# Attention and Fourier mixing on one core: banks taken by their planned readers, left-over frequencies of two batches together, half of the k sums on GpSimd, block 1 loaded earlier

## The chip, the core and the metric

The kernel runs on one core of one Trainium2 chip. A core has TensorE (PE in the profile; its weight loads are shown as PEld), VectorE (DVE), ScalarE (ACT), GpSimd (POOL) and SyncE (SP), each with its own in-order queue of instructions. They share an on-chip memory of 128 partitions, the PSUM banks that matmuls write, and 16 DMA engines. The metric is the device time of one execution in microseconds, a median of several runs.

## The reference, cut to what matters

There are 8 batches of 576 positions, 8 heads of 64. Each batch has two attentions, one over groups of four positions (pooled) and one in a band of seven positions (local). Their sum x goes through a real part of a two-dimensional Fourier transform, a normalization and a two-layer network with residual.

```python
q_d = q.reshape(B, H, Sd, 4, D).mean(axis=3)        # k_d and v_d likewise; Sd = 144
out_up = np.repeat(sm_attn(q_d, k_d, v_d), 4, axis=2)
mask = np.abs(pos[:, None] - pos[None, :]) < 4      # local attention
x = out_up + softmax(where(mask, q k^T / 8, -1e9)) @ v
u = x + np.real(np.fft.fft(np.fft.fft(x, axis=1), axis=2))
un = (u - mean(u)) / sqrt(var(u) + 1e-6)            # over 512 channels
out = u + np.maximum(un @ w_ch1, 0) @ w_ch2         # 512 -> 2048 -> 512
```

The weights of the network come as 64-bit floats and are turned into pairs of 32-bit parts (a high one and the rest) on the chip; matmuls of the transform and of the network are done with such pairs, so each product takes three matmuls.

## The kernel before, in words

**Attention.** For each batch, five units of the local attention (class Unit) load a window of q and k (`qkT`), compute banded scores (`sc`), row maxima, exponentials (`sb`), transposes (`tpl`, `pT`), values (`av`) and write their result to one of two x tiles. Beside them four pairs of heads of the pooled attention (class Pooled) do the same on sums of four positions: `sums` (of q and k, L385, on VectorE, a reduction of each unit's `qkT`), scores `sp`, exponentials `sd`, transposes `tp`, values `avd`, output `odt`. The pooled v comes as four loads that add into `vsum`, three of them through GpSimd's queue, each waiting for the one before (L263).

**Mixing.** Class Mix turns a batch's x into the transform. GpSimd adds two halves of channels (`pq`, L514, in three buffers), VectorE folds them (`xeo`, L524 and L525), ScalarE and GpSimd split the result into a high and a low part (`fh`, `fl`, L539). TensorE applies the sequence transform (`y`, L559; `yz`, L575) to 290 frequencies, split again into `yh` and `yl`. Then `mix` (L597) applies the channel transform to the frequencies in slots of 128, 128 and 34 columns (`outs`); each slot is 13 matmuls, 6 of the odd and 7 of the even part. ScalarE copies the odd part (`copy_odd`), VectorE joins it with the even one (`join`, L609), and SyncE's queue stores the two results to `um` in DRAM (L615, L616).

**Network.** Class Block has 9 blocks of 512 tokens in four tiles `ut`. A block loads three parts: the local output `ul` (L700), two halves of the transform `um` (L688) and the pooled output `ud` (L685), the latter two added by the DMA. Statistics (L707 to L711), normalization `un` (L718), transposes `tpn` (L726) and a split into `unT` follow. `hps` (L755) is the first layer of one of 16 parts of the hidden size, `acc` (L773 to L775) the second. Weights are fetched in 64 quarters (`raw`, L157) and decoded by ScalarE (L167), GpSimd (L172), VectorE (L180 to L186), ScalarE (L197) and GpSimd (L201). The weights' places in memory become free as the attention ends, in steps (close_b, close_a, close_e, close_d). Blocks 0 and 1 first take five hidden parts each, while the rest of the weights is decoded.

**What sets the order.** Each step is put on a list with a due time, `at(t, fn)`, in planner's units: a batch every 20 units (`PACE`), and offsets from the table `AT`. The list is sorted by due time, and the instructions of all engines are issued in that order; each engine then works through its own in order and waits where data or a buffer is not there. PSUM banks (8 up to the crossing, 4 in the network, where `acc` has the others) are given out in rotation:

```python
def bank(name, rows=P):
    banks.append(banks.pop(0))
    return banks[-1].tile([P, DM], F32, name=name, tag="ps")[:rows]
```

The tiles of block 0 are in memory from the beginning, and its loads are due within batches 3 and 4. The tiles of block 1 take a place that the attention holds until its end (close_a), so its loads are due after it.

Of the kernel before, what the change touches and what calls it, by code (L numbers as in the profile page):

```python
# [20 lines left out]
PACE = 20  # L21
AT = {
    "pooled": (1.03, 0.13, -1.91, -2.96, -3.43),
    "mix": (18.91, 18.7, 18.08),
    "local_steps": (0, 1.57, 2.96, 4.76, 5.59, 7.95, 9.34),
    "pooled_steps": (0.2, 1.79, 3.0, 4.98, 5.63, 7.67, 9.22),
    "qk": (-12.1, 2.19),
    "sums": (-2.36, 0.34),
    "sum_v": (-12.66, -6.03, -4.76, 2.6),
    "load_v": (2.43,),  # L30
    "store_pooled": (0.1, 0.13),
    "crosses": ((1, 4.04), (2, 7.41), (0, 9.2)),
    "folds": ((3, 5.99), (1, 4.28), (2, 8.33), (0, 10.12)),
    "splits": (0.74, 0.9, 1.59),
    "z": (9.57, 11.56, 13.47, 16.06),
    "sequence": (12.92, 1.78, 0.82, 1.66),
    "mixed": (20.18, 2.55, 0.47, 0.7, 1.51, 2.55),
    "store_local": (9.66,),
    "ffn": (3.56, 1.64),
    "decode": (49.49, 9.91, 9.02, 1.2, 1.84),  # L40
    "decode_steps": (-1.47, -0.47, 0.83, 2.01, 2.96),
    "first_norms": (89.93, -0.58, 91.0, 4.0),
    "second_norms": (0.03, 1.47, 0.8, 1.93),
    "add": (0, 2.77, 2.2),
    "add0": (59.9, 3.96, 6.0),
    "early": (3.97, 1.76),
    "constants": (15.12, 26.0),
    "qk1": (-12.1, 2.19),
    "sum_v1": (-11.31, -6.45, -2.94, 2.35),
# [21 lines left out]
def kernel(  # L71
# [27 lines left out]
    NK1 = 290  # L99
    GX = G - W  # L100
# [17 lines left out]
    res.tile([P, 104], F32, name="gap")  # L118
# [17 lines left out]
    uts = {0: [res.tile([P, DM], F32, name=f"ut0{i}") for i in range(TILES)]}  # L136
    unTs = {0: res.tile([P, 2, NCC, TILES * P], F32R, name="unT0")}
    stat = ctx.enter_context(tc.tile_pool(name="stat", bufs=4))
    mhalf = res.tile([P, 25], F32, name="mhalf")[:, :1]
# [79 lines left out]
    pbank = ExitStack()  # L219
    banks = [ctx.enter_context(tc.tile_pool(name="banks", bufs=8 - TILES, space=PSUM))]  # L220
    banks.append(pbank.enter_context(tc.tile_pool(name="more_banks", bufs=TILES, space=PSUM)))
    first_bank = banks[:1]
    pools = {}

    def bank(name, rows=P):
        banks.append(banks.pop(0))
        return banks[-1].tile([P, DM], F32, name=name, tag="ps")[:rows]
# [823 lines left out]
```

## Time and profile before

| | |
|---|---|
| median of 3 runs (lowest, highest) | 1157.84 us (1153.98, 1159.70) |
| profiled execution, its own time | 1156.91 us |
| its span, first to last instruction | 1155.1 us |
| PE busy, share of the span | 1088.4 us, 94% |
| DVE, ACT, POOL busy | 529.5, 352.7, 323.2 us |
| mean granted clock of TensorE | 0.964 |

Matmuls are pipelined, so a busy TensorE is one that has matmuls under way. PEclk is the granted clock as a share of 2.4 GHz; it has two levels, 1.2 and 2.4 GHz, so a mean of 0.89 is a stretch with some time at the lower one. `a <- b` in a list of waits reads: the instruction a waited until b was done. The tiles' names in the rows are those of the code above.

### The profile page before, as it was taken

How to read it: one execution, taken by the hardware profiler on the slowest of the kernel's cores; microseconds unless marked ns; L12 is line 12 of the kernel's file. 1: busy time of each engine (PE TensorE's matmuls, PEld its weight loads, DVE VectorE, ACT ScalarE, POOL GpSimd, SP SyncE). 2: the span in 40 equal slices, each digit the busy share in tenths (PEclk: the TensorE clock that was granted, in tenths of full speed). 3: DMA queues.
4: the chain of work that ended last, by engine and by line, in shares of the span. 5: the costliest groups of instructions: out<-in, count | busy, mean ns of one | idle time of the engine just before them, and what ended most of it. 6: DMA issues, size and time to landing. Idle time of an engine off the chain costs nothing.

```text
span 1155.1 us, 20852 instructions
## 1 busy us (share of the span) xinstructions
PE 1088.4 (94%) x8304; PEld 917.1 (79%) x8304; DVE 529.5 (46%) x1218; ACT 352.7 (31%) x1046; POOL 323.2 (28%) x447
## 2 busy tenths in 40 slices
PE   4889898899986999999999999999999999999998
PEld 3778787788865888888888888888888888888887
DVE  3778879898658999232222232232222122132111
ACT  2657746766633444111111111111111111111110
POOL 2124654432285656403202102301300400400000
PEclk6789879999987999999999999999999999999999
DMA  9677798677385444604204303302401501500000
GB/s 272 192 233 240 205 233 246 192 187 212 107 216 116 137 126 119 129 17 104 43 1 98 49 1 89 58 1 72 75 0 58 90 1 44 102 1 21 16 1 36
DMA packets 64338, 119.45 MB, mean 103 GB/s; under 512 B 8845, under 2 KB 22813, under 8 KB 63986
## 3 DMA queue, kind: packets, MB, share of 16 engines
q1 hardware_dynamic: 44706, 87.50, 23.9%
q0 software_dynamic: 19536, 30.62, 15.9%
q8 instruction: 65, 1.06, 0.4%
q14 instruction: 31, 0.25, 0.1%
HBM read 89.92 MB, written 27.05 MB: 101 GB/s over the span
## 4 chain that ended last, share of the span: by engine, by line
PE 68%; DVE 2%; POOL 1%; DMA 1%; issue 1%; SPq 0%; ACT 0%; DVEq 0%; POOLq 0%; ACTq 0%
PE hps L755 33%; PE acc L775 11%; PE acc L773 11%; PE acc L774 11%; PE tpn L726 1%; DMA raw<-in_wq_dram 1%; POOL ut L688 1%; DVE wt L183 0%; DVE ut L779 0%; DVE st L707 0%; DVE wt L180 0%; DVE un L718 0%; DVE o L609 0%; DVE unT L735 0%; PE mix L597 0%
## 5 line engine op out<-in xcount | busy, mean ns | idle before, releaser
L763 DVE SCALAR_TENSOR_TENSOR hl<-hps,hh 128x512 fp32r<-128x512 f32 x144 | 99.4, 691 | 472.9 <-ACT hh L759 472.8
L755 PE MATMUL hps<-unT,w1h 128*128 128x512 f32 x1152 | 311.8, 393 | 0.0
L755 PEld LDWEIGHTS hps<-unT,w1h 128*128 128x128 f32 x1152 | 214.1, 188 | 43.9 <-ACT w1h L197 0.3
L759 ACT ACTIVATE hh<-hps 128x512 fp32r<-128x512 f32 x144 | 85.8, 596 | 522.1 <-PE hps L755 519.9
L773 PE MATMUL acc<-w2h,hh 128*128 128x512 f32 x576 | 224.7, 390 | 0.0
L775 PE MATMUL acc<-w2h,hl 128*128 128x512 f32 x576 | 224.3, 389 | 0.0
L774 PE MATMUL acc<-w2l,hh 128*128 128x512 f32 x576 | 224.2, 389 | 0.0
L755 PE MATMUL hps<-unT,w1l 128*128 128x512 f32 x576 | 154.5, 390 | 1.8 <-POOL w1l L201 1.8
L688 POOL DMA_DIRECT2D ut<-um x96 | 84.5, 1511 | 204.4 <-DMA ut<-ul 169.9
L755 PEld LDWEIGHTS hps<-unT,w1l 128*128 128x128 f32 x576 | 108.0, 188 | 25.1 <-POOL w1l L201 2.2
L775 PEld LDWEIGHTS acc<-w2h,hl 128*128 128x128 f32 x576 | 108.2, 188 | 22.7
L773 PEld LDWEIGHTS acc<-w2h,hh 128*128 128x128 f32 x576 | 108.2, 188 | 22.3
L774 PEld LDWEIGHTS acc<-w2l,hh 128*128 128x128 f32 x576 | 108.3, 188 | 22.3
L711 POOL TENSOR_TENSOR rstd<-rstd,mhalf 128x1 f32<-128x1 f32 x36 | 20.1, 559 | 272.5 <-DVE rstd L710 272.4
L419 ACT ACTIVATE sb<-sc,mx 128x64 f32<-128x64 f32 x320 | 69.8, 329 | 1.3
L319 PE MATMUL avd<-vsum,ptd 72*72 72x65 f32 x512 | 43.3, 243 | 8.6 <-DMA vsum<-in_vg_dram 6.8
L559 PE MATMUL y<-seqm,fh 128*128 128x290 f32 (+1 forms) x256 | 45.7, 323 | 5.4 <-ACT fh L532 3.5
L735 DVE TENSOR_TENSOR unT<-tpn,unT 128x512 fp32r<-128x512 f32 x36 | 24.8, 689 | 56.5 <-ACT unT L732 56.5
L319 PEld LDWEIGHTS avd<-vsum,ptd 72*72 72x72 f32 x512 | 41.7, 159 | 9.8 <-issue 9.0
L385 DVE TENSOR_REDUCE sums<-qkT 128x256 f32<-128x1024 f32 (+5 forms) x48 | 43.4, 946 | 11.1 <-DMA qkT<-in_qk_dram 10.4
L539 POOL TENSOR_TENSOR fl<-xeo,fh 128x512 fp32r<-128x512 f32 (+1 forms) x32 | 40.8, 1279 | 25.0 <-ACT fh L532 14.2
L685 POOL DMA_DIRECT2D ut<-ud x40 | 46.6, 1820 | 1.7 <-DMA ut<-um 1.3
(90 smaller groups left out, 1325.1 us busy)
## 6 DMA issues: line engine op xcount, KB each, us to landing
qkT<-in_qk_dram SPq DMA_DIRECT2D x40, 512.0 KB
raw<-in_wq_dram SPq DMA_DIRECT2D x64, 256.0 KB
vaug<-in_vw_dram SPq DMA_DIRECT2D x40, 260.0 KB
out_dram<-ut SPq DMA_DIRECT2D x36, 256.0 KB
ul<-x SPq DMA_DIRECT2D x8, 1024.0 KB
ut<-ud POOLq DMA_DIRECT2D x32, 256.0 KB, 6.6
vsum<-in_vg_dram POOLq DMA_DIRECT2D x24, 292.5 KB, 6.4
ut<-um POOLq DMA_DIRECT2D x48, 128.0 KB, 4.5
```

The costliest lines, as they stand in the source:

```text
L319: nc.tensor.matmul(av[:, t, hl, :], self.pts[h0][hl][:, kt, t * GH : (t + 1) * GH], self.vs[:, kt, h0 + hl, :], start=(kt == 0), stop=(kt ...
L385: nc.vector.tensor_reduce(out=to[:, :, g : g + n], in_=groups, axis=AX.X, op=ALU.add)
L419: nc.scalar.activation(out=self.sb[:, hp, h2], in_=sc[:, hp], func=AF.Exp, scale=0.125, bias=self.mx[:, h2, hp : hp + 1],)
L559: nc.tensor.matmul(y, l, r, start=(i == 0), stop=(i == len(mms) - 1))
L685: nc.gpsimd.dma_start(out=u[to : to + m], in_=groups, accum_op=ALU.add)
L688: nc.gpsimd.dma_start(out=u[to : to + m, h * HD : h * HD + HD], in_=um[b][i, k + j : k + j + m, z : z + HD], accum_op=ALU.add,)
L755: nc.tensor.matmul(hps, a[:, c, :], unT[:, x, c, :], start=(i == 0), stop=(i == len(mms) - 1))
L759: nc.scalar.activation(out=hh, in_=self.hps[f], func=AF.Relu)
L763: nc.vector.scalar_tensor_tensor(out=hl, in0=self.hps[f], scalar=0.0, in1=self.hh[f].bitcast(F32), op0=ALU.max, op1=ALU.subtract)
L773: nc.tensor.matmul(acc, hh, w2h, start=start, stop=False)
L774: nc.tensor.matmul(acc, hh, w2l, start=False, stop=False)
L775: nc.tensor.matmul(acc, hl, w2h, start=False, stop=stop)
```

## The change

1. **Banks.** Each of the eight banks is a pool of its own. `bank()` takes the one whose last planned reader is due first, which it looks up in the list of due times.
2. **Left-over frequencies.** An even batch mixes two slots of 128 and keeps its last 34 columns of `yh`, `yl` and `yz` at the front of the same tiles (`keep_rest`, three ScalarE copies). The odd batch behind it mixes two slots of 128 and one that holds both batches' rest. Its store writes the rest of both. `pq` has one buffer instead of three and `o` one instead of two.
3. **Sums of k.** From batch 2 on, the k half of `sums` is done by GpSimd in two additions for each group of columns, and the q half by VectorE in a reduction of half the size. In batches 0 and 1 VectorE does both, in two instructions.
4. **Block 1.** Its tiles `ut` are in memory from the beginning, as block 0's are; its loads and statistics are due within batches 4 to 6, its normalization after close_e as before.
5. **Start.** The mask and the identity in bf16 are ScalarE copies of a load in 32 bit by SyncE's queue; before, GpSimd's DMAs cast them.
6. **Table.** Nearly all offsets of `AT` are new, with own ones for batches 0 and 1; the constants' loads are split in two.

```diff
 PACE = 20
+POOL_SUMS = ((slice(0, 4), 0), (slice(4, 8), 1))
 AT = {
-    "mix": (18.91, 18.7, 18.08),
+    "mix": (19.06, 17.6, 18.13),
...
-    "mixed": (20.18, 2.55, 0.47, 0.7, 1.51, 2.55),
+    "mixed": (21.92, 2.32, 0.48, 0.57, 1.64, 2.55),
-    "add": (0, 2.77, 2.2),
-    "add0": (59.9, 3.96, 6.0),
+    "add0": (61.1, 1.15, 5.8),
+    "add1": (78.68, 3.12, 6.41),
+    "norms1": (127.29, 3.83, 1.92, 1.93),
...
-    uts = {0: [res.tile([P, DM], F32, name=f"ut0{i}") for i in range(TILES)]}
+    uts = {n: [res.tile([P, DM], F32, name=f"ut{n}{i}") for i in range(TILES)] for n in range(2)}
...
-    nc.gpsimd.dma_start(out=identb, in_=c_ident)
-    nc.gpsimd.dma_start(out=maskb, in_=c_mask)
+    mask = raws[0][:, P : 2 * P]
+    nc.sync.dma_start(out=mask, in_=c_mask.rearrange("p n w -> p (n w)"))
+    nc.scalar.copy(out=identb, in_=ident)
+    nc.scalar.copy(out=maskb.rearrange("p n w -> p (n w)"), in_=mask)
...
+    def read_until():
+        if now[0] is None:
+            return -1e8
+        owner, name, args = place(now[0])
+        if name == "mix":
+            return times[(owner, "copy_odd" if args[1] else "join", args[:1])]
+        return times[(owner, readers[name], args)]
+
     def bank(name, rows=P):
-        banks.append(banks.pop(0))
-        return banks[-1].tile([P, DM], F32, name=name, tag="ps")[:rows]
+        free = min(banks)
+        free[:2] = read_until(), len(events) + (bank_uses.append(name) or len(bank_uses))
+        return free[2].tile([P, DM], F32, name=name, tag="ps")[:rows]
...
-                nc.vector.tensor_reduce(out=to[:, :, g : g + n], in_=groups, axis=AX.X, op=ALU.add)
+                for h, pool in POOL_SUMS:
+                    if pool and self.b > 1:
+                        two = p2.tile([P, HP, 32, 2], F32, name="two", bufs=1)[:, :, :n]
+                        nc.gpsimd.tensor_tensor(out=two, in0=groups[:, h, :, 0:2], in1=groups[:, h, :, 2:4], op=ALU.add)
+                        nc.gpsimd.tensor_tensor(out=to[:, h, g : g + n], in0=two[:, :, :, 0], in1=two[:, :, :, 1], op=ALU.add)
+                    else:
+                        nc.vector.tensor_reduce(out=to[:, h, g : g + n], in_=groups[:, h], axis=AX.X, op=ALU.add)
...
+    places = [
+        [(REST, P), (REST + P, P)],
+        [(2 * REST - 1, P), (2 * REST - 1 + P, P), (0, 2 * REST - 1)],
+    ]
...
-            pq = self.pq[t] = psq.tile([P, 2, HD], F32, name="pq", bufs=3)
+            pq = self.pq[t] = psq.tile([P, 2, HD], F32, name="pq", bufs=1)
...
+        def keep_rest(self):
+            for y in (self.yh, self.yl):
+                nc.scalar.copy(out=y[:, :, :REST], in_=y[:, :, NK1:].bitcast(F32))
+            nc.scalar.copy(out=yz[:34, :REST], in_=yz[:34, NK1:].bitcast(F32))
...
-            n = outs[t]
-            cols = slice(P * t, P * t + n)
+            first, n = places[self.b % 2][t]
+            cols = slice(first, first + n)
...
-                STORE.dma_start(out=u[2 * P : HS + 1], in_=self.o[:n, i, NSL - 1])
+                if k:
+                    STORE.dma_start(out=um[self.b - 1][i, 2 * P : HS + 1], in_=self.o[:n, i, 2])
+                    STORE.dma_start(out=u[:n], in_=self.o[REST : REST + n, i, 2])
...
-            at(t_a + AT["add"][1] + 0.1 * i + AT["add"][2] * part, blocks[1].load, i, part)
+    for n, begin in enumerate((0.0, t_e)):
+        first, step, step_part = AT[f"add{n}"]
+        first_s, step_s, first_n, step_n = AT[f"norms{n}"]
+        for i in range(TILES):
+            for part in range(3):
+                at(first + step_part * part + step * i, blocks[n].load, i, part)
+            at(first_s + step_s * i, blocks[n].stats, i)
+            blocks[n].prepare_rest(i, begin + first_n + step_n * i)
```

Three places show how instructions move. The first is GpSimd's queue between batch 1's last low parts `fl` and batch 2's first cross sum `pq`. Before:

```order
L539 TENSOR_TENSOR fl<-xeo,fh 128x512
L172 TENSOR_SCALAR wt<-wt 128x256
L539 TENSOR_TENSOR fl<-xeo,fh 128x512
L263 DMA vsum<-in_vg_dram 72x1040 x2
L201 TENSOR_TENSOR w1l_86<-wt,w1h_85 128x256
L172 TENSOR_SCALAR wt<-wt 128x256
L263 DMA vsum<-in_vg_dram 72x1040
L700 DMA ut_95<-ul_65 61x512
L700 DMA ut_95<-ul_65 57x512
L700 DMA ut_95<-ul_65 10x512
L514 TENSOR_TENSOR pq<-x_134 128x256 x2
```

After (L433 and L434 are the new additions, `two` their intermediate):

```order
L213 TENSOR_TENSOR w1l_85<-wt,w1h_84 128x256
L308 DMA vsum<-in_vg_dram 72x1040
L433 TENSOR_TENSOR two<-qkT 128x256
L434 TENSOR_TENSOR sums<-two 128x4x32
L433 TENSOR_TENSOR two<-qkT 128x4x56
L434 TENSOR_TENSOR sums<-two 128x4x28
...
L433 TENSOR_TENSOR two<-qkT 128x4x54
L434 TENSOR_TENSOR sums<-two 128x4x27
L184 TENSOR_SCALAR wt<-wt 128x256
L308 DMA vsum<-in_vg_dram 72x1040
L771 DMA ut_94<-ul_65 61x512
```

Twelve additions now stand there, the k sums of batch 3, between two loads into `vsum`; block 0's first loads follow as before.

The second is TensorE's queue after the attention, from the first layer of hidden part 2 of block 0 to block 1's first transposes `tpn`. Before:

```order
L755 MATMUL hps<-unT_99,w1h_5921 128x512 x4
L755 MATMUL hps<-unT_99,w1l_5922 128x512 x4
L755 MATMUL hps<-unT_99,w1h_5921 128x512 x4
L726 MATMUL tpn<-ident,un 128x128 x4
L597 MATMUL mix<-chanm,yh 128x258 x2
L597 MATMUL mix<-chanm,yl 128x258
L597 MATMUL mix<-chanm,yh 128x258 x2
L597 MATMUL mix<-chanm,yl 128x258
```

After (`acc` at L847 to L849 is the second layer, `hps` at L829 the first, `mix` at L663):

```order
L829 MATMUL hps<-unT_102,w1h_6060 128x512 x4
L829 MATMUL hps<-unT_102,w1l_6061 128x512 x4
L829 MATMUL hps<-unT_102,w1h_6060 128x512 x4
L847 MATMUL acc<-w2h_90,hh 128x512
L848 MATMUL acc<-w2l_91,hh 128x512
L849 MATMUL acc<-w2h_90,hl 128x512
...
L848 MATMUL acc<-w2l_91,hh 128x512
L849 MATMUL acc<-w2h_90,hl 128x512
L797 MATMUL tpn<-ident,un 128x128 x4
L663 MATMUL mix<-chanm,yh 128x258 x2
```

The twelve second-layer matmuls of hidden part 1 now stand ahead of the transposes; before they stood behind them and a slot of the mixing.

The third is SyncE's queue at the same place. Before:

```order
L622 DMA ul_72<-x_135 128x4x512
L623 DMA ul_72<-x_135 64x2x512
L157 DMA raw<-in_wq_dram 128x512 x3
L700 DMA ut_5917<-ul_65 7x512
L700 DMA ut_5917<-ul_65 56x512
...
L700 DMA ut_5920<-ul_66 1x512
L157 DMA raw<-in_wq_dram 128x512 x12
L615 DMA um_80<-o 128x2x258
```

After (L682 to L685 store `um`, L169 fetches `raw` weights, L691 and L692 store the last batch's local output):

```order
L682 DMA um_79<-o 128x2x258 x2
L691 DMA ul_72<-x_157 128x4x512
L692 DMA ul_72<-x_157 64x2x512
L169 DMA raw<-in_wq_dram 128x512 x17
L682 DMA um_80<-o 128x2x258
L684 DMA um_79<-o 33x258
L685 DMA um_80<-o 33x258
```

The 21 loads of block 1's local part (the rows from L700 on, of which four stand here) are gone from between the weight fetches.

## Rows read from the trace of the kernel before

**Rows 1.** Busy time by stage: us, busy (instructions) of each engine, clock, DMA share, GB/s.

```profile
0.00:62.00 62.00, 40.15 (x732) 35.04 (x732) 35.72 (x94) 30.86 (x117) 17.22 (x32) 0.75 0.79 234
62.00:200.00 138.00, 122.40 (x1924) 108.35 (x1921) 110.36 (x303) 88.21 (x325) 65.67 (x89) 0.89 0.83 233
200.00:318.00 118.00, 107.59 (x1975) 96.70 (x1973) 98.51 (x286) 81.91 (x302) 39.08 (x51) 1.00 0.61 173
318.00:372.60 54.60, 39.79 (x205) 33.27 (x196) 35.36 (x79) 18.30 (x47) 39.30 (x56) 0.81 0.68 164
372.60:1149.00 776.40, 776.40 (x3479) 642.35 (x3478) 246.81 (x457) 133.39 (x256) 161.95 (x220) 1.00 0.24 55
```

**Rows 2.** The chain that ended last, in order of time: start, us, what.

```profile
372.86 2.77 PE hps L755 x12
378.35 2.72 PE hps L755 x12
...
1149.09 2.73 DVE ut L779 x4
```

**Rows 3.** TensorE's waits, 62 to 318 us: us in total, times, longest; first and last.

```profile
PE sp L274 <- DVE x L467: 2.8, 5, 0.7
...
PE y L559 <- ACT fh L532: 0.3, 1, 0.3
```

**Rows 4.** TensorE in order of time, start: start, us, what, [idle before <- releaser].

```profile
8.38 0.43 PE L394 MATMUL sc<-maskb,identb 64*64 64x256 bf16 x4 [3.61 <-DMA maskb<-in_c_mask_dram]
...
28.62 2.15 PE L319 MATMUL avd<-vsum,ptd 72*72 72x65 f32 x16 [6.75 <-DMA vsum<-in_vg_dram]
```

**Rows 5.** TensorE in order of time, batch 0's slot of 34.

```profile
93.81 0.42 PE L597 MATMUL mix<-chanm,yh 128*34 128x258 f32 x2
...
95.39 0.60 PE L431 MATMUL tpl<-ident,sb 128*128 128x128 f32 x4
```

**Rows 6.** Groups by line: busy, mean ns. VectorE's sums, all, largest and smallest form.

```profile
L385 DVE TENSOR_REDUCE sums<-qkT 128x256 f32<-128x1024 f32 (+5 forms) x48 | 43.4, 946 | 11.1 <-DMA qkT<-in_qk_dram 10.4 <-DMA vaug<-in_vw_dram 0.3 <-PE sp L274 0.2
L385 DVE TENSOR_REDUCE sums<-qkT 128x256 f32<-128x1024 f32 x8 | 9.8, 1220 | 6.0 <-DMA qkT<-in_qk_dram 5.4 <-DMA vaug<-in_vw_dram 0.3 <-PE sp L274 0.2
L385 DVE TENSOR_REDUCE sums<-qkT 128x96 f32<-128x384 f32 x8 | 4.4, 544 | 0.2 <-DMA qkT<-in_qk_dram 0.2
```

**Rows 7.** Groups by line and form: joins on 34 rows, statistics.

```profile
L609 DVE TENSOR_TENSOR o<-mix,o 34x258 f32<-34x258 f32 x16 | 6.7, 417 | 2.5 <-ACT o L603 2.1
L707 DVE BATCH_NORM_STATS2 st<-ut 128x6 f32<-128x512 f32 x36 | 24.6, 685 | 5.0 <-DMA raw<-in_wq_dram 5.0
```

**Rows 8.** GpSimd's additions by line: ns min/median/max, first and last start.

```profile
L514 POOL TENSOR_TENSOR pq<-x x48: 623/633/1382, 49.2 to 322.9; 128x256 f32<-128x256 f32 x48
L539 POOL TENSOR_TENSOR fl<-xeo,fh x32: 1253/1274/1410, 53.8 to 329.3; 128x512 fp32r<-128x512 f32 x24, 80x512 fp32r<-80x512 f32 x8
```

**Rows 9.** VectorE's folds by line: ns min/median/max.

```profile
L524 DVE TENSOR_TENSOR xeo<-pq x24: 406/418/1498, 50.4 to 325.3; 128x256 f32<-128x256 f32 x24
```

**Rows 10.** TensorE in order of time, crossing into the network.

```profile
344.84 1.59 PE L755 MATMUL hps<-unT,w1h 128*128 128x512 f32 x4
354.53 1.12 PE L726 MATMUL tpn<-ident,un 128*128 128x128 f32 x4 [8.10 <-DVE un L718]
```

**Rows 11.** GpSimd in order of time: first and last DMA issues of block 1.

```profile
331.34 5.21 POOL L688 DMA_DIRECT2D ut<-um  x6
...
344.11 4.82 POOL L685 DMA_DIRECT2D ut<-ud  x5
```

**Rows 12.** GpSimd in order of time: last decoding step, first and last of 45.

```profile
376.64 0.74 POOL L201 TENSOR_TENSOR w1l<-wt,w1h 128x256 fp32r<-128x256 f32 x1 [1.33 <-ACT w1h L197]
...
463.49 0.74 POOL L201 TENSOR_TENSOR w2l<-wt,w2h 128x256 fp32r<-128x256 f32 x1 [0.80 <-ACT w2h L197]
```

**Rows 13.** DMA issues: KB each, median us to landing.

```profile
ut<-um POOLq DMA_DIRECT2D x48, 128.0 KB, 4.5
```

**Rows 14.** TensorE in order of time: last scores of a batch, first of the next.

```profile
229.31 0.88 PE L274 MATMUL sp<-sums 64*72 64x144 f32 x8
...
242.40 0.71 PE L274 MATMUL sp<-sums 64*72 64x144 f32 x8 [0.70 <-DVE x L467]
```

More of the change, by code (lines that the diff above doesn't have):

```diff
@@ L99 @@
     NK1 = 290
+    REST = NK1 - 2 * P
     GX = G - W
@@ L219, with place @@
     pbank = ExitStack()
-    banks = [ctx.enter_context(tc.tile_pool(name="banks", bufs=8 - TILES, space=PSUM))]
-    banks.append(pbank.enter_context(tc.tile_pool(name="more_banks", bufs=TILES, space=PSUM)))
-    first_bank = banks[:1]
+    stacks = [ctx] * (8 - TILES) + [pbank] * TILES
+    banks = [[-1e9, i, x.enter_context(tc.tile_pool(name=f"bank{i}", bufs=1, space=PSUM))] for i, x in enumerate(stacks)]
+    first_banks = banks[: 8 - TILES]
     pools = {}
+    bank_uses, now = [], [None]
+    readers = {
+        "scores": "exps",
+        "transpose_p": "copy_p",
+        "values": "result",
+        "sequence": "sequence_low",
+        "sequence_z": "z_low",
+        "turn": "turn_low",
+        "first": "low",
+    }
+    times = {}
+    def place(fn):
+        return getattr(fn.func, "__self__", None), fn.func.__name__, fn.args
+    def read_until():
[5 more added lines that the diff above has]
+        return times[(owner, readers[name], args)]
     def bank(name, rows=P):
-        banks.append(banks.pop(0))
-        return banks[-1].tile([P, DM], F32, name=name, tag="ps")[:rows]
+        free = min(banks)
+        free[:2] = read_until(), len(events) + (bank_uses.append(name) or len(bank_uses))
+        return free[2].tile([P, DM], F32, name=name, tag="ps")[:rows]
     xab = [px.tile([P, NSL, 2, DM + 2], F32, name=f"x{i}") for i in range(2)]
@@ L636, in plan @@
-            at(t + AT["store_local"][0], self.store_local)
+                u = max(t + pace * u, moved if slot >= NSL - 1 else 0)
+                at(u + pace * fold, self.fold, slot)
+                at(u + pace * high, self.split_high, slot)
+                at(u + pace * low, self.split_low, slot)
+            at(t + pace * AT["store_local"][0], self.store_local)
             for d, fn in zip(AT["z"], (self.split_z, self.sequence_z, self.z_high, self.z_low)):
-                at(t + d, fn)
+                at(t + pace * d, fn)
@@ L639, in plan @@
             first, step, high, low = AT["sequence"]
             for T in range(4):
-                u = t + first + step * T
+                u = t + pace * (first + step * T)
                 at(u, self.sequence, T)
-                at(u + high, self.sequence_high, T)
-                at(u + low, self.sequence_low, T)
+                at(u + pace * high, self.sequence_high, T)
+                at(u + pace * low, self.sequence_low, T)
             first, step, even, copy, join, store = AT["mixed"]
-            for i in range(NSL):
-                u = t + first + step * i
+            if self.b % 2 == 0:
+                at(t + pace * AT["keep"][0], self.keep_rest)
@@ L648, in plan @@
+            for i in range(len(places[self.b % 2])):
+                u = t + pace * (first + step * i)
                 at(u, self.mix, i, 1)
-                at(u + even, self.mix, i, 0)
-                at(u + copy, self.copy_odd, i)
-                at(u + join, self.join, i)
-            at(u + store, self.store)
+                at(u + pace * even, self.mix, i, 0)
+                at(u + pace * copy, self.copy_odd, i)
+                at(u + pace * join, self.join, i)
+            at(u + pace * store, self.store)
@@ L834, in close_a @@
         pools["pt"] = pool("pt")
-        uts[1] = [pools["pt"].tile([P, DM], F32, name=f"ut1{i}") for i in range(TILES)]
         weight_tiles(pools["pt"], range(*CHUNKS[:2]))
         pbank.close()
-        banks[:] = first_bank
+        banks[:] = first_banks
         pacc[0] = pool("pacc", TILES, space=PSUM)
@@ L900 @@
     with tc.manual_schedule():
+        times.update((place(fn), t) for t, _n, fn in events)
         for _, _n, fn in sorted(events, key=lambda e: e[:2]):
+            now[0] = fn
             fn()
```

147 lines of the change are left out of this document (77 added, 70 removed).

## The prediction

> **What bounds the kernel now.** I read the busy times by stage first. They divide the run into a start (0 to 62 us), an attention part in two halves (62 to 200, 200 to 318), a crossing into the feed-forward network (318 to 372.6) and the network itself [rows 1]. The reader is to see that in the last stage TensorE is busy for all of its 776.4 us at clock 1.00. The chain of waits says the same: groups of 12 matmuls, 2.72 us each, one behind another up to the closing additions [rows 2]. 12 matmuls in 2.72 us are 0.227 us each, and the change takes none of them away. So whatever it brings must come out of the first 372.6 us.
>
> There TensorE stands still for 62 - 40.15 = 21.9 us in the start, (138 - 122.40) + (118 - 107.59) = 26.0 us in the attention, and 54.6 - 39.79 = 14.8 us in the crossing [rows 1]. It also runs slowly: the granted clock is 0.89 between 62 and 200 us. With its two levels, 1.2 and 2.4 GHz, that is 0.11 / 0.5 x 138 = 30 us at the lower one, against none between 200 and 318. VectorE is nearly as full as TensorE there (110.36 + 98.51 of 256 us, 82%). The list of TensorE's waits in the attention then tells who holds it up: 18 kinds of wait, the longest 2.8 us in total [rows 3]; 12 of the 18 name VectorE as the one that ended them, 17.0 us together. No single wait is worth much. The attention is four engines closely interleaved, and a gain must come from less work on the two full ones.
>
> **The change part by part.**
>
> *The left-over frequencies.* Before, each batch turns 290 frequencies in three slots of 128, 128 and 34 rows, and the slot of 34 costs 13 matmuls like a full one. At full clock it runs from 93.81 to 95.39, 1.58 us [rows 5]. Now an even batch has two slots and the odd one behind it three, so four of eight such slots go: 4 x 1.58 = **6.3 us** of TensorE, on the path. VectorE loses four pairs of joins on 34 rows, 8 x 0.417 = 3.3 us [rows 7]. ScalarE gains three small copies for each pair of batches and loses one; it is busy for (88.21 + 81.91) / 256 = 66% [rows 1], so I cost that at nothing, and at the 3 us it may take in all if ScalarE should be late.
>
> *The sums of k on GpSimd.* VectorE spends 43.4 us on 48 reductions, 5.43 us a batch [rows 6]. From the two ends, 1.220 us for 1024 elements and 0.544 for 384, an element costs 1.06 ns and an instruction 0.14. Half the elements of each then saves (5.43 - 6 x 0.14) / 2 = 2.3 us a batch, 13.8 us over six batches; batches 0 and 1 pay 6 x 0.14 each for the split, 1.7 us. Block 1's four statistics move into the attention, 4 x 0.685 = 2.7 us [rows 7]. VectorE's net relief is 13.8 + 3.3 - 1.7 - 2.7 = 12.7 us of the 209 that it is busy.
>
> How much of that reaches TensorE the trace doesn't show. Nothing is the lower bound, and the upper one is the 17.0 us of waits that VectorE ends. The new choice of PSUM banks (the bank whose planned last reader is earliest, in place of strict rotation) works on the same waits, since many of the 17 us are for a reader of an older tile. I take **8 us** for the two together, a little under half of the 17, since a wait that goes leaves the next one behind it.
>
> GpSimd takes on 12 additions a batch, 1152 + 576 = 1728 elements. Its addition of 256 elements takes 0.633 us and that of 512 takes 1.274 [rows 8], 2.5 ns an element, so 4.3 us a batch, or 6 us with some wait between dependent instructions. Is there room? The first scores of a batch follow the last ones of the batch before: 229.31 + 0.88 to 242.40 is 12.2 us [rows 14]. So in itself it is hidden. The cover goes where the instructions ahead of it in GpSimd's queue are late: the sums of batches 4 and 5 stand behind accumulating DMAs of blocks 0 and 1, of which six hold GpSimd for 5.21 us [rows 11] and each lands 4.5 us later [rows 13]. I charge **-6 us** for this, for the single buffer of pq (the next cross sum must wait for VectorE's fold), and for block 0's first read of the left-over rows, which the plan puts 0.4 of its units behind the store that writes them. Bounds: 0 and -40, the latter being a whole 6 to 7 us a batch on the path.
>
> One thing speaks against moving work to GpSimd: a fold on VectorE, 0.418 us as a rule, took 1.498 in one case [rows 9], with GpSimd's cross sums beside it. The Trainium skill states the reason on the page "SBUF — State Buffer", section "Who interferes with whom": a VectorE instruction with two SBUF inputs and a GpSimd one that reads SBUF exclude each other for the whole instruction. The trace agrees as far as that one row goes. By that rule the folds would pay wherever the sums stand beside them, and I make a rival of it below; the sum keeps the row's median, because in the new order the twelve additions stand between two batches' cross sums and folds, not among them.
>
> *The clock.* Between 200 and 318 us, with few idle gaps, it never fell; between 62 and 200 it was low for 30 us, in which TensorE could have done its work in half the time. The upper bound is 15 us, the lower 0. Fewer waits should take some of that; I take **5 us**.
>
> *The start.* The mask comes by SyncE's queue and a ScalarE copy instead of a casting DMA of GpSimd. TensorE's first wait for it was 3.61 us, and the longest of the start, 6.75 us, is for the accumulated v sums [rows 4]. In the new order more local work stands ahead of that wait: four units' scores, three transposes and two value products instead of three, one and one. But the DMA engines are busy for 0.79 of this stage [rows 1], and the loads are as many as before. I take **4 us**, bounds -3 and 12.
>
> *The crossing.* Before, the loads of block 1 wait for the end of the attention: GpSimd issues its DMAs from 331.34 until 344.11 + 4.82 = 348.9 [rows 11], its weight decoding waits between them, and TensorE, done at 344.84 + 1.59 = 346.4, starts block 1's first transposes at 354.53 after 8.10 us [rows 10]. From 346.4 to the next block's first group at 378.35 [rows 2] are 31.9 us. The work in it is 60 matmuls of the network (5 x 2.72 = 13.6), 39 of the mixing (39 x 1.58 / 13 = 4.7) and 16 short transposes (about 0.9): 19.2. So 12.7 us are idle or slow. With block 1 loaded long before, its statistics are there, and a group of 12 second-layer matmuls stands ahead of the transposes. What is late next is the decoding of weights: 45 quarters take from 376.64 to 463.49 when nothing is in their way, 1.97 us each [rows 12]. From 329 on, the 12 quarters of this round would be done by about 353, and TensorE needs the last of them some ten us after 346. So decoding should hold little. I take **10 us**, bounds 4 and 12.7.
>
> *The sum.* 6.3 + 8 - 6 + 5 + 4 + 10 = 27.3 us. The profiled execution took 1156.9 us (span 1155.1 and 1.8 around it; the median of the three runs, 1157.8, is 0.1% from it), so 1156.9 - 27.3 = **1130 us**. With the bounds of the parts near their better ends together it would be 1107, and with most near their worse ends 1145.
>
> **The rivals.**
>
> *A: the attention keeps its pace.* The in-order queues hand each freed wait to the next engine, so only the removed matmuls and the crossing count: 1156.9 - 6.3 - 10 + 3 = 1144. For it: the 18 small waits. Against it: VectorE is the releaser in most.
>
> *B: the clock stays up.* With most of VectorE's waits gone, TensorE never falls to 1.2 GHz in the attention: 13 of the 17 us, 12 of the 15, and the start's 8 instead of 4: 27.3 + 5 + 7 + 4 = 43 less, 1114. For it: the stretch from 200 to 318. Against it: twice the loads into the network's blocks in this part.
>
> *C: the shared port.* If GpSimd's additions do fall beside VectorE's eight folds a batch, and each waits as in the longest row, 8 x 1.08 x 6 = 52 us come onto VectorE in place of 12.7 off it. Half of the net 39 us on the path and the 8 us lost: 1130 + 8 + 19 = 1157.
>
> *D: slower.* GpSimd's sums come late at the first scores of every batch, since they stand behind DMAs that wait for landings. The price is the wait there, six times; from 27 / 6 = 4.5 us a batch on, all else is eaten up. At 7 us beyond my charge: 1130 + 42 = 1172. For it: the landings of 4.5 us that stand in the same queue [rows 13]. Against it: the 12.2 us of room [rows 14].
>
> *E: the change doesn't do what it says at the crossing*: decoding, not block 1, holds it. Then it returns 3 instead of 10: 1137, inside the forecast's own range.
>
> **How the numbers follow.** The forecast with E has 0.52 (its own range 1119 to 1140), A 0.18, B 0.13, C 0.07, D 0.10. For 8 in 10 I take 1108 to 1152: it leaves out D, most of C and the tail of B. About 0.5% is what a measurement of this kernel can tell from no change, here 5.8 us, so faster means under 1152. The forecast, A and B lie there but for a tail: 0.82. Between 1152 and 1163.6 lie most of C and the tails of A and D: 0.09. Slower: 0.09.
>
> **What would show it.** The network's part must again be about 776 us. The end of the attention (the last value products, at 318 before) should come near 301 us, and the dense part begin near 346 instead of 373. In the list of waits, TensorE's wait for VectorE's un of 8.10 us must be gone. VectorE's reductions must shrink to about 31 us, GpSimd's new additions sum to 26 to 40 us. The mixing must have 260 matmuls instead of 312. A wait of the first scores (sp) for GpSimd's sums of over 4 us in most batches would show D; folds with a median over 0.8 us would show C; an attention that still ends beyond 312 us would show A.

## The result and the profile after

The changed kernel takes 1142.3 us (median of 4 runs, 1139.9 to 1145.5) against 1157.6: a ratio of 0.987, 95% interval 0.983 to 0.991. That is faster by 15.3 us where 27.3 were forecast: inside the range, but nearer to rival A (1144) than to 1130. The profiled execution took 1144.4 us, with a span of 1142.3. One execution further below, of e11, took 3695 us where the others took 1140 to 1143, and its ratio leaves it out.

Busy time by stage, after, in the columns of [rows 1]:

```profile
0.00:62.00 62.00, 48.47 (x809) 40.17 (x810) 39.47 (x115) 35.40 (x133) 17.67 (x32) 0.83 0.89 273
62.00:200.00 138.00, 117.68 (x1895) 103.36 (x1895) 95.71 (x288) 85.36 (x317) 95.49 (x148) 0.90 0.86 230
200.00:318.00 118.00, 111.24 (x1878) 99.15 (x1879) 96.56 (x301) 83.61 (x309) 56.85 (x87) 0.94 0.68 185
318.00:360.00 42.00, 39.66 (x215) 34.19 (x214) 32.98 (x69) 19.34 (x50) 23.47 (x38) 0.96 0.50 150
360.00:1136.00 776.00, 773.12 (x3449) 637.39 (x3448) 238.93 (x447) 128.42 (x250) 159.74 (x216) 1.00 0.24 54
```

The reader is to see three things. In the crossing TensorE is now nearly always busy (39.66 of 42 us; before 39.79 of 54.6). In the attention VectorE is busy for 16.6 us less (192.27 against 208.87) and GpSimd for 47.6 more (152.34 against 104.75), yet TensorE idles as much as before: (138 - 117.68) + (118 - 111.24) = 27.1 us against 26.0. And its clock there is no better: 0.90 and 0.94 against 0.89 and 1.00.

TensorE in order of time, after, where [rows 10] stood: the first network matmuls behind the attention, the first transposes of block 1, and the group that stood at 378.35 [rows 2]:

```profile
316.08 1.20 PE L829 MATMUL hps<-unT,w1h 128*128 128x512 f32 x4
...
341.99 0.60 PE L797 MATMUL tpn<-ident,un 128*128 128x128 f32 x4
...
364.87 1.07 PE L829 MATMUL hps<-unT,w1h 128*128 128x512 f32 x4
```

The same two groups of network matmuls before, by the same view:

```profile
318.06 1.20 PE L755 MATMUL hps<-unT,w1h 128*128 128x512 f32 x4
...
378.19 1.07 PE L755 MATMUL hps<-unT,w1h 128*128 128x512 f32 x4
```

So the attention ends 2.0 us earlier and the crossing is 60.1 - 48.8 = 11.3 us shorter. The wait of 8.10 for `un` is gone; TensorE's waits from 312 to 380 us, after, are these two:

```profile
PE y L617 <- ACT fh L590: 1.5, 1, 1.5
PE yz L641 <- POOL z L606: 0.8, 1, 0.8
```

The rest of the span is the same to half a microsecond (777.4 against 776.9). The question is why the start and the attention, where 17 us were forecast together, gave 2.

TensorE's waits in the attention, 62 to 318 us, after (us in total, times, longest), to be held against [rows 3]:

```profile
PE y L617 <- POOL fl L597: 4.3, 2, 3.8
PE yz L641 <- POOL z L606: 3.8, 1, 3.8
PE tpn L797 <- DVE un L789: 3.0, 1, 3.0
PE sc L445 <- ACT sb L470: 3.0, 5, 1.1
...
PE sp L319 <- POOL sums L434: 0.6, 1, 0.6
```

GpSimd, which ended none of the 18 kinds of wait before, now ends 8.7 us of them. The sums that it took over are hardly among these (0.6 us); `fl` and `z` are, which were its work before too.

### The profile page after: what moved, and what is told of

The parts are those of the page before. It is cut to its first block, busy times and chain, and to the rows that moved or that the text cites. A ratio compares the mean times of both kernels' runs of the same rounds, so it can differ in the third digit from the quotient of the medians.

```text
span 1142.3 us, 20905 instructions
## 1 busy us (share of the span) xinstructions
PE 1092.7 (96%) x8252; PEld 916.1 (80%) x8252; DVE 506.4 (44%) x1222; ACT 352.1 (31%) x1057; POOL 353.2 (31%) x517
## 4 chain that ended last, share of the span: by engine, by line
PE 72%; DMA 12%; DVE 7%; POOL 4%; ACT 3%; issue 2%; SPq 1%; POOLq 0%; ACTq 0%; DVEq 0%
PE hps L829 30%; PE acc L849 10%; PE acc L847 10%; PE acc L848 10%; DMA raw<-in_wq_dram 4%; DMA vsum<-in_vg_dram 4%; DMA qkT<-in_qk_dram 2%; PE y L617 2%; PE mix L663 2%; PE tpn L797 1%; PE avd L364 1%; DMA ut<-um 1%; PE av L499 1%; DVE sums L436 1%; DVE x L518 1%
## 5 line engine op out<-in xcount | busy, mean ns | idle before, releaser
L829 PE MATMUL hps<-unT,w1h 128*128 128x512 f32 x1152 | 310.9, 392 | 0.0
L829 PEld LDWEIGHTS hps<-unT,w1h 128*128 128x128 f32 x1152 | 213.9, 188 | 43.1
L847 PE MATMUL acc<-w2h,hh 128*128 128x512 f32 x576 | 225.7, 392 | 2.9 <-DVE ut L853 2.8
L849 PE MATMUL acc<-w2h,hl 128*128 128x512 f32 x576 | 225.1, 391 | 0.0
L829 PE MATMUL hps<-unT,w1l 128*128 128x512 f32 x576 | 154.3, 390 | 0.0
L847 PEld LDWEIGHTS acc<-w2h,hh 128*128 128x128 f32 x576 | 108.5, 188 | 27.1 <-ACT w1h L209 2.0
L849 PEld LDWEIGHTS acc<-w2h,hl 128*128 128x128 f32 x576 | 108.5, 188 | 23.9 <-DVE hl L837 1.3
L829 PEld LDWEIGHTS hps<-unT,w1l 128*128 128x128 f32 x576 | 108.1, 188 | 23.1
L782 POOL TENSOR_TENSOR rstd<-rstd,mhalf 128x1 f32<-128x1 f32 x36 | 21.0, 643 | 265.6 <-DVE rstd L781 261.7
L597 POOL TENSOR_TENSOR fl<-xeo,fh 128x512 fp32r<-128x512 f32 (+1 forms) x32 | 44.9, 1411 | 23.6 <-ACT fh L590 21.6
L179 ACT ACTIVATE wt<-raw 128x256 f32<-128x256 f32 x64 | 28.1, 439 | 62.1 <-DMA raw<-in_wq_dram 44.9
L803 ACT CAST unT<-tpn 128x512 fp32r<-128x512 f32 x36 | 21.1, 587 | 82.0 <-PE tpn L797 82.0
```

Source lines behind the costliest of these rows:

```text
L597: nc.gpsimd.tensor_sub(out=l, in0=self.x[t], in1=h.bitcast(F32))
L829: nc.tensor.matmul(hps, a[:, c, :], unT[:, x, c, :], start=(i == 0), stop=(i == len(mms) - 1))
L847: nc.tensor.matmul(acc, hh, w2h, start=start, stop=False)
L849: nc.tensor.matmul(acc, hl, w2h, start=False, stop=stop)
```

## The experiments

In this table "end" is the start of the first network matmuls behind the attention and "crossing" the time from there to the group named above, by TensorE in order of time. Both are of one profiled execution each; the median and the ratio are of all. Ratios are to the kernel before, run on the same chip. e4 and e5 leave out part of the work, as said there.

| kernel | end | crossing | median | ratio (95%) |
|---|---|---|---|---|
| before | 318.06 | 60.1 | 1157.6 | 1 |
| after | 316.08 | 48.8 | 1142.3 | 0.987 (0.983 to 0.991) |
| e1 sums back | 327.92 | 49.7 | 1153.0 | 0.997 (0.995 to 0.999) |
| e2 block 1 late | 304.25 | 70.8 | 1152.9 | 0.998 (0.996 to 0.999) |
| e3 block 1 mid | 322.25 | 47.2 | 1148.5 | 0.993 (0.991 to 0.995) |
| e4 no left-over slot | 311.74 | 47.7 | 1141.8 | 0.988 (0.986 to 0.990) |
| e5 block 1 thin | 306.31 | 47.3 | 1132.0 | 0.980 (0.977 to 0.983) |
| e6 block 1 spread | 316.53 | 55.0 | 1150.3 | 0.995 (0.994 to 0.997) |
| e7 banks alone | 319.59 | 58.5 | 1155.7 | 0.999 (0.997 to 1.001) |
| e8 sums alone | 321.21 | 60.0 | 1160.4 | 1.004 (1.002 to 1.006) |
| e9 slots back | 315.41 | 48.6 | 1145.7 | 0.990 (0.987 to 0.992) |
| e10 block 1 tail | 315.79 | 53.7 | 1148.6 | 0.992 (0.989 to 0.994) |
| e11 rows by SyncE | 315.44 | 49.0 | 1142.7 | 0.986 (0.983 to 0.989) |
| e12 reads behind | 308.32 | 49.4 | 1138.3 | 0.986 (0.983 to 0.989) |

**e1**, the changed kernel with the sums on VectorE:

```diff
-POOL_SUMS = ((slice(0, 4), 0), (slice(4, 8), 1))
+POOL_SUMS = ((slice(0, 8), 0),)
```

> All sums of k go back to VectorE, one reduction for all eight heads as before the change; everything else stays as after the change (1142 us). VectorE takes on again about 14 us over six batches, GpSimd loses 34 us. Theory L (the loads of both blocks crowd the DMA engines and GpSimd's queue between 94 and 228 us, and the attention goes at their pace there): VectorE has room in that stretch (35.5 us busy of 50), so it costs little, 1140 to 1145. Rival S (the sums on GpSimd hold back its fl, z and vsum; 8.1 us of TensorE's waits name POOL): those waits go, 1134 to 1138. The prediction's own step (relief of VectorE reaches TensorE at a good half): 1147 to 1152.

It lost 0.0096 of the ratio, 11 us, all of it in the attention (11.8 us longer). So VectorE's relief does reach TensorE, and more of it than the prediction took; rival S of the expectation falls, and theory L's figure for this run was wrong too.

**e2**, block 1's loads, statistics and norms at their old places behind the attention (three due times).

> The loads, statistics and norms of block 1 go back to their places behind the attention, as before the change; the rest stays. The crossing should take its 11.5 us again. Theory L: the attention is rid of block 1's transfers, its last value products come near 309 instead of 316, so 1142 + 11.5 - 7 = 1147. Rivals S and P (TensorE's own work and clock set the pace of the attention): the attention still ends at 316 and the whole is 1153 to 1154.

The attention ended at 304.25, 11.8 us earlier, and nothing else was taken out of it: block 1's loads and statistics cost what the sums gained. The whole was 1153 nevertheless, since the crossing took 70.8 us, 22.0 more than after the change and 10.7 more than before it. TensorE's waits in it, 316 to 376 us:

```profile
PE hps L829 <- POOL w1l L213: 8.2, 1, 8.2
PE tpn L797 <- DVE un L789: 7.7, 2, 7.3
```

That is the old wait for `un` and a second one, for a decoded weight in GpSimd's queue behind the loads (before, TensorE's waits of that kind came to 1.8 us). So in the new order the early loads pay 0.0103 of the ratio, 12 us, although by place they take from the attention as much as the crossing gained over the kernel before. Theory L was right in its direction on the attention (304 where it said 309) and too low on the crossing.

**e3**, the loads later inside the attention:

```diff
-    "add1": (78.68, 3.12, 6.41),
+    "add1": (108.0, 3.12, 6.41),
-    "norms1": (127.29, 3.83, 1.92, 1.93),
+    "norms1": (141.0, 3.83, 1.92, 1.93),
```

> The loads of block 1 stay inside the attention but start some 60 us later (plan 108 instead of 78.68, about 2.1 us a unit), where the DMA engines are less full (0.66 and 0.36 after 262 us, against 0.99 and 0.92 between 130 and 228); the statistics follow at 141. Theory L: at least half of the 9 us that the stretch from 94 to 228 lost comes back, 1135 to 1138. Rivals S and P: 1141 to 1143. If the statistics now come late for the crossing: 1144 to 1150, with TensorE waiting for un there.

Worse by 6 us. Up to 217 us it kept pace with e2 (the start of batch 4's `yz`, 217.55 there and 216.70 in e2); then it lost, where the loads now stood, and ended 18.0 us behind e2. So the price went with them and grew, and theory L's hope of room failed.

**e4**, the odd batches without the slot of 67 rows (rows of another slot are stored in their place, so this work is left out):

```diff
-        [(2 * REST - 1, P), (2 * REST - 1 + P, P), (0, 2 * REST - 1)],
+        [(2 * REST - 1, P), (2 * REST - 1 + P, P)],
...
```

> Odd batches leave out the slot of 67 left-over frequencies of two batches (rows of another slot are stored in their place): 4 x 13 matmuls, 4 copies and 8 joins less than after the change. Rival P (TensorE's work sets the pace): 4 x 1.58 = 6.3 us less, 1136. Theory L: the slots of batches 1 and 3 stand in the crowded stretch and return little, those of 5 and 7 return 3.2: 1139. Theory S: the same as L. If nothing in the attention is TensorE's: 1142.

In the profiled execution the attention was 4.3 us shorter, but over the runs the time did not differ from after (intervals 0.986 to 0.990 and 0.983 to 0.991).

**e5**, to part the transfers from the queue: block 1's accumulating loads move 4 rows each. Block 1's result thereby leaves out most of the mixed and pooled parts; every instruction stays.

```diff
+                    s = 4 if self.n == 1 else m
...
-                            out=u[to : to + m, h * HD : h * HD + HD],
+                            out=u[to : to + s, h * HD : h * HD + HD],
...
```

> The accumulating loads of block 1 alone are cut to 4 rows each (block 1's result leaves out the rest of the mixed and pooled parts); every instruction, wait and queue stays, only about 2 MB of transfers go. With block 1's loads behind the attention (e2_block1_late) the attention's last value products ended near 304 us, after the change at 316. Theory T (the transfers themselves: the DMA engines are 0.99 busy from 130 to 180 us): the attention ends at 304 to 308 and the whole takes 1130 to 1135. Rival Q (GpSimd's queue: issuing and waiting for a landing between two additions to one tile): the attention still ends at 313 to 316, 1139 to 1142. In between if both.

The attention ended at 306.31, 9.8 of e2's 11.8 us earlier, and the time fell to 0.980. GpSimd's queue was as full as after, and it waited no less for landings; its issues in 62 to 318 us (busy, mean ns, idle before them), after and then e5:

```profile
L759 POOL DMA_DIRECT2D ut<-um x22 | 20.7, 1404 | 1.5 <-DMA ut<-um 1.0 <-issue 0.4
```

```profile
L761 POOL DMA_DIRECT2D ut<-um x22 | 20.3, 1310 | 2.2 <-DMA ut<-um 2.0 <-issue 0.2
```

What changed were the DMA queues of 130 to 228 us (packets, MB, share of the 16 engines' time), after and then e5:

```profile
q1 hardware_dynamic: 8010, 16.07, 53.6%
q0 software_dynamic: 4368, 6.56, 41.0%
```

```profile
q1 hardware_dynamic: 9080, 18.43, 60.5%
q0 software_dynamic: 3089, 4.52, 27.8%
```

Two MB more on GpSimd's queue took 13.2% of 98 us, 12.9 us of all DMA engines, and in the same stretch SyncE's queues, which feed the attention, moved 2.4 MB less. The engines were full either way (0.95 and 0.89 over the stretch). The Trainium skill says on the page "DMA: Bandwidth & Descriptors", section "SWDGE vs HWDGE vs iDMA", that each DMA engine goes in turn through inner queues, some fed by software and some by hardware; the trace agrees in that what one kind gained the other lost, though any sharing of full engines would show that.

**e6**, the loads later still and further apart:

```diff
-    "add1": (78.68, 3.12, 6.41),
+    "add1": (124.0, 3.12, 9.5),
-    "norms1": (127.29, 3.83, 1.92, 1.93),
+    "norms1": (157.0, 1.5, 1.92, 1.93),
```

> Block 1's loads as a whole, but later still and further apart: plan 124 with 9.5 between the three parts (about 250 to 305 us) and the statistics at 157 (about 305 to 312 us), where after the change the DMA engines are 0.66 busy (262 to 295) and 0.36 (295 to 316). Theory T (cost by lack of transfer room): most of the 11.8 us comes back, the attention ends at 304 to 309, 1131 to 1136. Rival: block 1 costs about the same wherever it stands inside the attention, as in e3_block1_mid (1148): 1142 to 1149. If the statistics now come late for block 1's first transposes: TensorE waits for un again in the crossing.

A miss: 1150. The loads now fell among batch 7's loads of q and k. The first of GpSimd's waits from 240 to 316 us, by its total, and the next batch's sums with it:

```profile
POOL two L433 <- DMA qkT<-in_qk_dram: 10.7, 3, 8.3
```

That wait fits the attention's end, which came no earlier than after the change (316.53). The 6.2 us that e6 lost to the changed kernel stand in the crossing, where TensorE waits from 300 to 376 us for the last batch's `z`:

```profile
PE yz L641 <- POOL z L606: 6.0, 1, 6.0
```

GpSimd shows the reason. Four small steps of block 1's late statistics (`rstd`, L782, the last at 318.52) stand in its queue ahead of the last batch's `pq`, `fl` and `z`, and `z` comes at 328.07 where it came at 322.36 after the change.

**e7** and **e8** put one part each into the kernel before. e7 takes the new `bank` with its list of readers; e8 the loop over `POOL_SUMS` and, for room, `pq` in two buffers.

> The kernel before with one part of the change alone: each PSUM bank is the one whose planned last reader is earliest, instead of strict rotation; order and all else as before (1157 us). The prediction gave 8 us to this and to VectorE's relief together. If the rule is worth something by itself: 1150 to 1154. If it needs the new order: 1156 to 1159. If waits on an older tile were never what held TensorE: 1157.

> The kernel before with one part alone: half the heads' sums of k on GpSimd from batch 2 on (and two buffers of pq instead of three, for room). Taking this part out of the changed kernel cost 10.7 us (e1_sums_back). If VectorE's 14 us are what the attention goes by in the old order too: 1145 to 1149. If the gain needs the new order, where block 0's loads and the sums were given places that fit: 1154 to 1158. If GpSimd's queue becomes the wait: over 1160.

The banks by themselves gave nothing that can be told from no change. The sums, with the smaller `pq`, made the kernel slower, though VectorE is relieved as in the changed kernel (192.7 us busy from 62 to 318). TensorE's first wait in the list of 62 to 318 us in e8:

```profile
PE sp L275 <- POOL sums L390: 9.7, 4, 5.0
```

This is rival D, in the old order: the sums stand behind other work in GpSimd's queue, and the first scores wait, though for 2.4 us in the mean and not for over 4 in most batches. In the new order that wait is 0.6 us. What the buffer taken from `pq` costs wasn't parted from it.

**e9**, the four slots of 34 rows put back into the even batches:

```diff
-        [(REST, P), (REST + P, P)],
+        [(REST, P), (REST + P, P), (REST + 2 * P, REST)],
```

> The changed kernel (ratio 0.987 to the kernel before) with the four slots of 34 rows put back into the even batches as work alone: 13 matmuls, a copy and two joins each, their rows stored nowhere. By the prediction's step they cost 4 x 1.58 = 6.3 us: 1148 to 1149, ratio 0.993. If TensorE's work in the attention is covered by other engines' waits there, as e4_no_rest (four slots fewer, 1142 us) says: 1142 to 1144, ratio 0.987 to 0.989.

Up by 0.0023, some 2.7 us, with intervals that overlap; between the two expectations, and under half of the 6.3. The profiled execution ended its attention no later (315.41), so a price of the slots is not shown.

**e10**, block 1's loads behind the last loads of q and k:

```diff
-    "add1": (78.68, 3.12, 6.41),
+    "add1": (137.0, 2.0, 6.0),
-    "norms1": (127.29, 3.83, 1.92, 1.93),
+    "norms1": (162.5, 1.2, 1.92, 1.93),
```

> Block 1's loads as a whole, put behind the last batch's loads of q and k: plan 137, steps of 2 and 6 (about 272 to 306 us), where the changed kernel's DMA engines are busy for 0.50 (270 to 285) and 0.18 (300 to 316); statistics at 162.5 (about 312 us). e6_block1_spread had its first part just among those loads of q and k (plan 124 to 133), and its sums waited 8.3 us for one of them. Theory T, now narrower (block 1's transfers cost what they delay the next batch's loads of q and k): nothing of batch 7 is delayed, the attention ends at 303 to 308 as without block 1's transfers, and the whole takes 1130 to 1136. If block 1 costs the same wherever it stands: 1142 to 1150. If it lands too late for the crossing: TensorE waits for un, 1136 to 1144.

A miss again, 1149. TensorE's first waits from 252 to 326 us:

```profile
PE yz L641 <- POOL z L606: 6.9, 2, 3.5
PE tp L345 <- DVE odt L379: 1.8, 1, 1.8
PE y L617 <- POOL fl L597: 1.7, 1, 1.7
```

In the changed kernel `z` costs 0.8 us there. This time it is GpSimd's queue. One of the two waits is at 290.50, since `z` and `fl` of batch 6 stand among the issues of block 1's loads. The other is in the crossing, at 325.03, behind `rstd` as in e6, 2.7 us longer than after the change, of the 4.9 that the crossing lost. So the narrower theory (only delayed loads of q and k) doesn't cover it; a late place has a price of its own in the queue.

**e11** tries to take both kinds of price off block 0: its plain loads go by SyncE.

```diff
-                    eng = nc.sync if self.n else nc.gpsimd
-                    eng.dma_start(out=u[to : to + m], in_=ul[b][n // 2, j, r : r + m, :])
+                    nc.sync.dma_start(out=u[to : to + m], in_=ul[b][n // 2, j, r : r + m, :])
```

(`even_rows` now applies to block 0 too.)

> The changed kernel (ratio 0.987) with block 0's plain loads of the local rows issued by SyncE, as block 1's are, instead of by GpSimd: 12 issues of 0.6 us leave GpSimd's queue, and 1 MB goes by the hardware queues. Between 110 and 230 us of the changed kernel these moved 19.1 MB in 51.5% of the DMA engines' time, GpSimd's own 7.6 MB in 37.5%, so 1 MB takes 3.2 us on the one and 5.9 on the other. Theory T (transfers): 2.7 us less, and some of the GpSimd waits: 1137 to 1140, ratio 0.983 to 0.985. If SyncE's queue, now with 22 more short issues ahead of loads of q and k, delays these: 1142 to 1148, ratio 0.987 to 0.992.

No difference from after. TensorE's longest wait of 62 to 318 us, 9.5 us until 148.12, is for an `fl`; GpSimd in order of time shows why:

```profile
143.51 3.26 POOL L759 DMA_DIRECT2D ut<-um  x4 [5.44 <-DMA um<-o]
145.69 2.37 POOL L597 TENSOR_TENSOR fl<-xeo,fh 128x512 fp32r<-128x512 f32 x1
```

The read of the left-over rows waits for the store of them, and `fl` stands behind it in the queue.

**e12** is e11 with these reads behind that `fl`:

```diff
-    "add0": (61.1, 1.15, 5.8),
+    "add0": (61.1, 1.15, 7.3),
```

> e11_rows_sync (ratio 0.986) with block 0's reads of the mixed parts 1.5 units later in the plan: in GpSimd's queue the first read of left-over rows now stands behind the last fl of batch 2 instead of ahead of it, and batch 4's sums of k ahead of the reads of the pooled part. In e11 that read waited 5.4 us for the store of the left-over rows, and TensorE 9.5 us for the fl behind it. If that place in the queue is what ate e11's gain: TensorE's wait goes, 1133 to 1138, ratio 0.979 to 0.983. If the transfers alone set the pace there, the wait turns up elsewhere: 1140 to 1144, ratio 0.985 to 0.988.

The wait went from 9.5 to 2.2 us at most, and in the profiled execution (1135.5 us) the attention ended at 308.32:

```profile
PE tp L345 <- DVE odt L379: 3.5, 3, 2.4
PE y L617 <- POOL fl L597: 3.2, 3, 2.2
```

But its six runs spread from 1133.5 to 1146.5, and the ratio is that of e11. Whether it beats the changed kernel is left open; no version that was run does so beyond its interval with the whole work done.

## Why the prediction was right in sign and wrong in size

- **The step that failed** is the crossing's: "I take 10 us", with block 1 "loaded long before". The 10 were right by place (11.3), but the transfers that moved were given no price in the attention. Their place in GpSimd's queue was part of the 6 us charged with the sums; what they take of the DMA engines was put at nothing. The early loading costs 11.8 us there (e2), of which 9.8 go with the transfers (e5); the other 2 are the queue and the statistics, not parted. That there are twice as many loads stood only as a point against rival B. The row that should have been priced was in [rows 1]: DMA engines 0.83 busy from 62 to 200 us, into which 3 MB were put. Without them the attention ends at 304.25, near the 301 foretold. Most of the price stands between the first `yz` of batch 3 and that of batch 4. The stretch from one to the other after, in e2 and in e5, in the columns of [rows 1]:

```profile
181.83:227.58 45.75, 41.58 (x599) 36.83 (x600) 32.90 (x96) 28.15 (x101) 30.84 (x45) 0.79 0.91 228
```

```profile
180.23:216.70 36.47, 34.92 (x600) 31.28 (x600) 32.35 (x96) 28.04 (x101) 19.90 (x32) 0.95 0.67 190
```

```profile
180.70:218.14 37.44, 35.90 (x600) 32.09 (x600) 32.36 (x96) 28.10 (x101) 30.00 (x45) 0.92 0.78 227
```

  Of the 9.3 us that e2 is shorter here, 2.6 are idle time of TensorE; the other 6.7 are the same 600 matmuls taking longer at the lower clock. For e5, 8.3 us shorter, these are 2.6 and 5.7.
- **VectorE's relief and the banks, 8, less GpSimd's 6.** Too small: 2 net by the prediction, 11 to 12 net in the new order for the sums alone (e1). How much of that is more relief and how much a smaller charge isn't parted; GpSimd's additions took 34.3 us, inside the 26 to 40, and VectorE's reductions 29.8 for the 31 foretold [rows 6]. Groups by line, after, whole run:

```profile
L436 DVE TENSOR_REDUCE sums<-qkT 128x128 f32<-128x512 f32 (+5 forms) x60 | 29.8, 544 | 16.7 <-DMA qkT<-in_qk_dram 14.6 <-PE sp L319 2.0
...
L433 POOL TENSOR_TENSOR two<-qkT 128x256 f32<-128x256 f32 (+5 forms) x36 | 21.8, 606 | 4.9 <-DMA qkT<-in_qk_dram 3.0
L434 POOL TENSOR_TENSOR sums<-two 128x128 f32<-128x128 f32 (+5 forms) x36 | 12.5, 348 | 4.3 <-DMA raw<-in_wq_dram 1.6
```

  The banks alone gave 0 (e7). The old rotation under the new order wasn't tried, so what the rule is worth there stays open.
- **The slots, 6.3.** Too high: 2.7 by the medians of e9, which the intervals do not tell from nothing, and four slots fewer still give nothing that the runs can tell (e4). That TensorE's own work in the attention is covered by waits that stay would explain it; it is not shown. The mixing has 260 matmuls, as foretold.
- **The clock, 5.** Wrong in sign. At the lower of two levels (1.2 and 2.4 GHz) TensorE ran for (0.10 x 138 + 0.06 x 118) / 0.5 = 41.8 us from 62 to 318, against 30.4 before. In e5, where the accumulating transfers are gone, the two stretches show 0.94 and 1.00, 16.6 us. The prediction took fewer waits for a better clock, but the sum of idle time doesn't foretell it: in [rows 1] TensorE idled for 11% of the first stretch and 9% of the second, at 0.89 and 1.00, and from 62 to 200 us e5 idled for 23.4 us at 0.94 where the changed kernel idled for 20.3 at 0.90. What the rows do show is a place. After the change the clock was 0.50 from 205 to 215 us, right behind a wait of 3.0 for `un` (until 202.41) that neither e2 nor e5 has between those two `yz`. So the clock was not a gain to count apart from block 1's loads.
- **The start, 4.** Nearly right: the first `yz` came 2.8 us earlier (59.38 for 62.14), the mask's wait is gone and that for the sums of v fell from 6.75 [rows 4] to 1.4. A wait for ScalarE's `sb` came in their place. TensorE's waits, 0 to 62 us, after:

```profile
PE tpl L482 <- ACT sb L470: 7.5, 2, 6.5
...
PE avd L364 <- DMA vsum<-in_vg_dram: 1.4, 1, 1.4
```

- **The rivals.** A has the time (1144) and its sign (an attention ending beyond 312 us), but not its reason: the sums on GpSimd gain 11.8 us there (e1), and a loss of 11.8 (e2) hides it. B falls with the clock. C falls: the folds' median is 420 ns as before [rows 9], though one took 2.17 us. The longest folds stood beside `fl` for all but their end, not beside cross sums as the prediction read [rows 9], nor beside the new sums: before, a fold of 1.49 us ended at 59.37 and the `fl` at 59.06; after, the one of 2.17 us ended at 60.43 and the `fl` at 60.14. VectorE's folds, after (ns min/median/max):

```profile
L582 DVE TENSOR_TENSOR xeo<-pq x24: 406/420/2172, 49.5 to 323.6; 128x256 f32<-128x256 f32 x24
```

  By the rule of the Trainium skill (page "SBUF — State Buffer", section "Who interferes with whom") a fold, with two inputs, would be held by an addition of GpSimd beside it; the trace agrees in three folds after (2.17, 1.50 and 1.29 us), which end 0.3 us behind an `fl`, and in no median, since the new sums stand elsewhere. D did not come in the new order and came in part in the old (e8). E falls: decoding held nothing in the crossing.
- **The account of the span.** Crossing -11.3, network +0.5 and the time up to the attention's end -2.0 make -12.8 of 1155.1. That -2.0 is not a sum of the parts above: with the start's -2.8, the sums' -11.8 and the loads' +11.8 it should be -2.8 or better. The terms of e1 and e2 are taken from the changed kernel with one part undone, so they needn't add up exactly. The start (us) of each batch's first `yz` shows where the lead was lost:

| | batch 0 | 1 | 2 | 3 | 4 | end |
|---|---|---|---|---|---|---|
| before | 62.14 | 101.80 | 139.62 | 184.96 | 226.00 | 318.06 |
| after | 59.38 | 94.05 | 137.63 | 181.83 | 227.58 | 316.08 |
| e2 | 58.99 | 94.09 | 137.47 | 180.23 | 216.70 | 304.25 |
| e5 | 58.11 | 92.72 | 136.15 | 180.70 | 218.14 | 306.31 |

  At batch 1 the changed kernel led by 7.8 us. It lost 4.7 from batch 3 to 4, which e2 and e5 don't lose, and 5.8 from batch 1 to 2, which they lose too. So the second loss is not block 1's. It isn't the sums' either, since e1 takes 45.8 us there (after 43.6, before 37.8). Only e12, which moves block 0's loads, took under 41 in the new order (39.8). What causes this loss was not tried and stays open.
- **The sum's outer values.** 1107 and 1145 are not added up from the bounds that the parts were given. All better ends make 63 us, 1094; the worse ends, with GpSimd's charge left at 6, make 1 us, 1156.

## What to carry to other kernels

A load that is moved out of a stall may not be free where it lands, and here it was not: read the DMA share of the stretch that takes it, and price it by the queue's own time per MB there. Work that moves to a second engine needs a place in that engine's queue that fits who waits for it; nearly the same edit gave 11 us in one order and took 0.4% in another. When a large gain seems to vanish, undo the parts one at a time before calling the waits incompressible: two large terms may cancel.

## What the runs showed of the hardware that was not expected

- A MB on GpSimd's DMA queue, mostly accumulating loads, took 0.41 x 98 / 6.56 = 6.1 us of all 16 engines; one on SyncE's queues 0.536 x 98 / 16.07 = 3.3.
- GpSimd's time to issue these loads did not fall when block 1's moved 4 rows in place of up to 128 (20.7 and 20.3 us for 22 issues), so that time says nothing of what the transfers cost the DMA engines.
- The clock can carry the larger part of a stall's price: of the 9.3 us by which the changed kernel is longer than e2 from batch 3 to 4, 2.6 were idle and 6.7 slower matmuls.
